# Starting a chunk's q preparation twelve attention units before its first use, in place of ten

## The chip, the cores and the metric

The kernel runs on one core of one Trainium2 chip. The metric is the device time of one execution in microseconds (us). The kernel before took 984.87 us (median of three runs, 982.25 to 988.37). One more execution was profiled; its numbers are used wherever a stage or an instruction is spoken of.

## The reference

Four batches, eight heads, 768 positions, head size 64. Attention lets a query see only the keys whose nearest centroid (of sixteen per head, by cosine) is the query's own; the attention output, 3072 rows of 512, then goes through an MLP with 2048 hidden columns and a squared ReLU.

```python
q_assign = np.argmax(np.einsum('bhsd,hcd->bhsc', q_n, c_n), axis=-1)
k_assign = np.argmax(np.einsum('bhsd,hcd->bhsc', k_n, c_n), axis=-1)
mask = q_assign[:, :, :, None] == k_assign[:, :, None, :]
scores = np.where(mask, scale * np.matmul(q, k.transpose(0, 1, 3, 2)), -1000000000.0)
attn = softmax(scores)                      # exp after subtracting the row maximum
x = (attn @ v).transpose(0, 2, 1, 3).reshape(B * S, H * D)
r = np.maximum(x @ w_in, 0.0)
out = (s * (r * r) + b) @ w_out
```

All of it is float32. The kernel works with pairs of float16 tiles, a high part and the remainder, so a product costs two or three matmuls.

## The kernel before, in words

**Units and steps.** Attention is cut into 192 units, each 128 queries of one head against all 768 keys. A chunk is 256 positions of one batch, so a batch has three chunks of 16 units and lasts 48 units. A chunk's q is prepared in two halves of four heads each; a half serves 8 units and is called a q group here (24 of them, numbered u = 0 to 23; group u serves units 8u to 8u+7). The MLP of a chunk is cut into 16 steps, one for each 128 hidden columns, 192 in all, and MLP step m is written into the same pass of the main loop as unit m + 21.

**One pass i of the main loop** (the `while` near the end of the function) writes: the scores of unit i (L456: two matmuls of QA by KA, then two of QB by KB, into `sc`, which has two buffers); output matmuls of an MLP step (L602, `acc`); the float16 copy of unit i-1's probabilities (L119, `ph`); the row maximum on VectorE (L465) and exp on ScalarE (L472, L475) of unit i; the input matmuls of an MLP step (L575, `h`, one PSUM bank) and its ReLU and squares on ScalarE (L582 to L585), which need the chunk's scale `cf`; the remainder of `ph` on GpSimd (L498) and its DMA transpose `PT` (L500); the remainder of `g` on GpSimd (L590); in every second pass the matmuls with v (L517 to L519, `px`) and their evacuation on VectorE (L525 to L529). Last comes `background()`, which advances every preparation in progress by one stage, up to its next `yield`.

**A q group's preparation** (`prep_q`) has eight stages and so takes eight passes: 1 load of `qn` (SP queue); 2 absolute maximum (VectorE, L101); 3 the maximum over partitions (PE `am_q` and VectorE L98, PSUM bank `m`); 4 seven small scale instructions on VectorE (L68 to L70, L362 to L64) and the high split on ScalarE (L185); 5 the remainder split on VectorE (L187), a copy on GpSimd (L375) and the DMA transpose `QA` (L379); 6 nothing; 7 matmuls with the centroids (`pq`, L388 and L389, bank `m`) and the first two one-hot instructions (L288, L289); 8 the other four (L291 to L294) and the DMA transpose `QB` (L392). The scores of the group's first unit need QA and QB, each of which has two buffers.

**Other background work.** For batches 1 to 3, `prep_k` of four head pairs begins at passes 48b-20, 48b-16, 48b-12 and 48b-8 with the same eight stages (and bank `m`), and `prep_v` begins at 48b-20. `finish_x` turns every four units' output into the MLP's input: first an absolute maximum (VectorE) in a pass that is 3 modulo 4, then, one pass later, a remainder on GpSimd and the transpose `x` (L546); after a chunk's last head pair also the maximum over partitions `am_x`, in passes 20, 36, 52 and so on (16n+20). `mlp_start`, one pass after that, turns `am_x` into `cf` with small VectorE instructions (L560 to L566). Bank `m` is one buffer shared by `px`, `am_q`, `am_k`, `am_v`, `am_x`, `pq` and `pk`.

**What sets the order.** The kernel says what is computed, and in which order it is written; a scheduler with a simulated clock then fixes each engine's instruction order, by order of writing where it can, and adds the waits. On the chip each engine runs its own list in that order. Loads are ordered behind the latest `PT` transpose on SP. In the first 24 units the weights are also loaded, checked and split (`weights`, `wsplit`), with VectorE at work most of the time.

Of the kernel before, what the change touches and what calls it, by code (L numbers as in the profile page):

```python
# [26 lines left out]
def tile_cluster_attention_mlp(ctx, tc, q, k, v, cent, w_in, w_out, s_in, b_in, out):  # L27
# [7 lines left out]
    NCH = T // CT  # L35
# [363 lines left out]
    def prep_v(b):  # L399
        vm = sb.tile([P, 8], F32, tag="vm", name=f"vm_{b}", bufs=2)  # L400
        VM[b] = vm
        vns = []
        for hp in range(NP):
            vn = sb.tile([P, 2, T, D], F32, tag="kv", name=f"vn_{b}_{hp}", bufs=5)
            load(vn, v[b, 2 * hp : 2 * hp + 2].rearrange("h (p t) d -> p h t d", t=T), False)
            vns.append(vn)
            if b == 0:
                VN[hp] = vn
            yield
        for hp in range(NP):  # L410
            absmax(vm[:, hp : hp + 1], vns[hp].rearrange("p h t d -> p (h t d)"))
            if hp < NP - 1:
                yield
        vc = columns(1, f"v{b}")
        V.tensor_reduce(vc, vm[:, 0:NP], axis=AX.X, op=ALU.max)
        if b:
            yield
        allmax(vm[:, 5:6], vc, f"v{b}")
        yield
        floor2(V, vm[:, 6:7], vm[:, 5:6])  # L420
        inverse2(V, vm[:, 7:8], vm[:, 6:7], 0)
        V.tensor_scalar(vm[:, 7:8], vm[:, 7:8], 2.0 ** 13, None, op0=ALU.mult)
        V.tensor_scalar(vm[:, 6:7], vm[:, 6:7], 2.0 ** -19, None, op0=ALU.mult)
        for hp in range(NP):
            vh = sb.tile([P, 2, T, D + 2], F16, tag="vh", name=f"vh_{b}_{hp}", bufs=5)
            vl = sb.tile([P, 2, T, D], F16, tag="vl", name=f"vl_{b}_{hp}", bufs=5)
            VS[(b, hp)] = (vh, vl)
            G.memset(vh[:, :, :, D:], 1.0)
            yield from split(vh[:, :, :, :D], vl, vns[hp], vm[:, 7:8], False)
            if hp < NP - 1:  # L430
                yield
                if b > 0:
                    yield
                    yield
# [184 lines left out]
    def at(step, gen):  # L619
        later.setdefault(step, []).append(gen)  # L620
# [8 lines left out]
    for b in range(B):  # L629
        for c in range(NCH):  # L630
            for hq in range(2):
                s0 = ((b * NCH + c) * 2 + hq) * 8 - 10
                if s0 > 0:
                    at(s0, prep_q(b, c, hq))
        if b > 0:
            for hp in range(NP):
                at(48 * b - 20 + 4 * hp, prep_k(b, hp))
            at(48 * b - 20, prep_v(b))
# [122 lines left out]
```

## Time and profile before

| | |
|---|---|
| time, median of three | 984.87 us (982.25 to 988.37) |
| profiled execution, its own time | 987.78 us |
| its span | 986.0 us |
| granted TensorE clock over the span | 0.941 |
| PE, ACT, DVE, POOL busy | 85%, 74%, 68%, 56% |
| first scores of unit 32 | about 208 us into the span |
| last scores of unit 191 | about 906 us into the span |

PE is TensorE, DVE VectorE, ACT ScalarE, POOL GpSimd and SP the queue that issues all DMAs here; PEld is the loading of weights into TensorE, beside its matmuls. A group's row in the profile gives how many instructions it has, their busy time in us, the mean of one in ns, and then the time for which the engine stood idle just before them with what ended that. Rows of a stage view give its length and each engine's busy time with the number of instructions.

### The profile page before, as it was taken

How to read it: one execution, taken by the hardware profiler on the slowest of the kernel's cores; microseconds unless marked ns; L12 is line 12 of the kernel's file. 1: busy time of each engine (PE TensorE's matmuls, PEld its weight loads, DVE VectorE, ACT ScalarE, POOL GpSimd, SP SyncE). 2: the span in 40 equal slices, each digit the busy share in tenths (PEclk: the TensorE clock that was granted, in tenths of full speed). 3: DMA queues.
4: the chain of work that ended last, by engine and by line, in shares of the span. 5: the costliest groups of instructions: out<-in, count | busy, mean ns of one | idle time of the engine just before them, and what ended most of it. 6: DMA issues, size and time to landing. Idle time of an engine off the chain costs nothing. (4 is left out here: it accounts for less than half of the span.)

```text
span 986.0 us, 22497 instructions
## 1 busy us (share of the span) xinstructions
PE 834.3 (85%) x8625; PEld 580.2 (59%) x8625; DVE 673.0 (68%) x1475; ACT 726.4 (74%) x1416; POOL 550.2 (56%) x543
## 2 busy tenths in 40 slices
PE   0568524887899999998799999997889999999997
PEld 0347312654566666765566666765666666767764
DVE  7798889989687665658787756578867567473100
ACT  4476776877578788867678877876788977789443
POOL 3125755556456576655467656655566766667322
PEclk9955566999999999999999999999999999999999
DMA  6865883687678775698888767797888676777200
GB/s 181 204 196 158 222 210 90 138 194 134 128 144 163 156 161 123 140 210 154 171 164 156 169 132 156 138 203 181 138 160 173 151 119 142 142 138 149 44 23 21
DMA packets 450299, 147.36 MB, mean 149 GB/s; under 512 B 417936, under 2 KB 446608, under 8 KB 450192
## 3 DMA queue, kind: packets, MB, share of 16 engines
q1 hardware_dynamic: 450192, 145.93, 69.7%
q8 instruction: 67, 1.10, 0.5%
q14 instruction: 40, 0.33, 0.1%
HBM read 35.69 MB, written 6.29 MB: 43 GB/s over the span
## 5 line engine op out<-in xcount | busy, mean ns | idle before, releaser
L498 POOL TENSOR_TENSOR ph<-p,ph 128x768 f16<-128x768 f32 x184 | 308.6, 1677 | 170.7 <-ACT ph L119 135.8
L575 PE MATMUL h<-x,wis 128*128 128x256 f16 x2304 | 292.0, 275 | 17.3 <-ACT r L582 12.2
L602 PE MATMUL acc<-wos,g 128*128 128x512 f16 x1152 | 295.4, 380 | 4.7 <-POOL g L590 2.9
L575 PEld LDWEIGHTS <-wis 128*128 128x128 f16 x2304 | 223.1, 98 | 74.9 <-issue 16.6
L590 POOL TENSOR_TENSOR g<-r,g 128x256 f16<-128x256 f32 x192 | 133.3, 695 | 139.7 <-ACT r L585 129.8
L465 DVE TENSOR_REDUCE ssm<-sc 128x1 f32<-128x768 f32 x192 | 180.9, 950 | 16.2 <-PE sc L456 16.0
L475 ACT ACTIVATE p<-sc,ssm,qsm 128x768 f32<-128x768 f32 x192 | 188.1, 980 | 3.9 <-DMA PT<-ph 1.8
L602 PEld LDWEIGHTS <-g 128*128 128x128 f16 x1152 | 104.1, 98 | 88.2 <-POOL g L590 6.9
L119 ACT ACTIVATE ph<-p 128x768 f16<-128x768 f32 x174 | 144.8, 832 | 11.1 <-DMA PT<-ph 10.8
L472 ACT ACTIVATE ssm<-ssm,lift,qsm 128x1 f32<-128x1 f32 x192 | 73.4, 382 | 101.9 <-DVE ssm L465 101.4
L517 PE MATMUL px<-vh,PT 128*128 128x65 f16 x1104 | 119.9, 196 | 14.5 <-DVE ksm L98 5.2
L582 ACT ACTIVATE r<-h,cf 128x256 f32<-128x256 f32 x192 | 89.1, 464 | 55.0 <-PE h L575 50.8
L518 PE MATMUL px<-vl,PT 128*128 128x64 f16 x1104 | 119.9, 193 | 0.0
L519 PE MATMUL px<-vh,PT 128*128 128x65 f16 x1104 | 119.9, 194 | 0.0
L456 PE MATMUL sc<-KA,QA 128*128 128x384 f16 x384 | 101.1, 343 | 20.2 <-ACT p L475 16.9
L518 PEld LDWEIGHTS <-PT 128*128 128x128 f16 x1104 | 103.6, 100 | 21.2 <-issue 12.8
L517 PEld LDWEIGHTS <-PT 128*128 128x128 f16 x1104 | 103.9, 98 | 17.5 <-issue 9.1
L456 PE MATMUL sc<-KB,QB 128*128 128x384 f16 x384 | 100.2, 345 | 7.8 <-DMA QB<-qb 7.7
L519 PEld LDWEIGHTS <-PT 128*128 128x128 f16 x1104 | 103.6, 98 | 3.0
L584 ACT ACTIVATE g<-r 128x256 f16<-128x256 f32 x192 | 79.5, 414 | 3.8
L585 ACT ACTIVATE r<-r 128x256 f32<-128x256 f32 x192 | 79.1, 412 | 3.3
L525 DVE TENSOR_SCALAR ssm<-px 128x2 f32<-128x2 f32 x92 | 14.2, 155 | 88.3 <-PE px L519 88.2
(153 smaller groups left out, 1090.9 us busy)
## 6 DMA issues: line engine op xcount, KB each, us to landing
wst<-in_moe_w_in_dram SPq DMA_DIRECT2D x16, 512.0 KB, 4.5
wst<-in_moe_w_out_dram SPq DMA_DIRECT2D x16, 512.0 KB, 4.1
kn<-in_k_dram SPq DMA_DIRECT2D x16, 384.0 KB, 3.9
qn<-in_q_dram SPq DMA_DIRECT2D x24, 256.0 KB, 3.8
vn<-in_v_dram SPq DMA_DIRECT2D x16, 384.0 KB, 4.4
out_dram<-o SPq DMA_DIRECT2D x12, 512.0 KB, 3.2
PT<-ph SPq DMA_TRANSPOSE x184, 3.4
x<-xn SPq DMA_TRANSPOSE x48, 2.5
```

Of the source, the lines that this page charges most:

```text
L119: A.activation(dst, src, AF.Copy)
L456: last_score[0] = nc.tensor.matmul(sc[:, e, :HALF], X[:, col, :], y[:, h * S + e * HALF : h * S + (e + 1) * HALF], start=st, stop=not st)
L465: last_max[0] = V.tensor_reduce(SM[i // 4][:, 0, j : j + 1], U[i]["sc"], axis=AX.XY, op=ALU.max, negate=True)
L475: last_exp[0] = A.activation(p.rearrange("p (a b) -> p a b", a=2), u["sc"], AF.Exp, bias=bi, scale=u["scale"], **total)
L498: G.tensor_tensor(u["ph"][:, 1, :], u["p"], u["ph"][:, 0, :], op=ALU.subtract)
L517: nc.tensor.matmul(o1, PT[:, kt, :], vh[:, h, kt, : D + 1], start=(kt == 0), stop=False)
L518: nc.tensor.matmul(o, PT[:, kt, :], vl[:, h, kt, :], start=False, stop=False)
L519: nc.tensor.matmul(o1, PT[:, T + kt, :], vh[:, h, kt, : D + 1], start=False, stop=(kt == T - 1))
L575: nc.tensor.matmul(ph[:, :CW], WSP[ft][0][:, wl, kt, :], XS[(b, c, kt)][:, :, xl, :], start=(i == 0), stop=(i == len(terms) - 1))
L582: A.activation(r, ph[:, :CW], AF.Relu, scale=MS[(b, c)][0])
L590: G.tensor_tensor(g[:, 1, :], r, g[:, 0, :], op=ALU.subtract)
L602: nc.tensor.matmul(acc[:, t, :], g[:, gl, rows], WSP[ft][1][:, wl, :], start=(ft == 0 and gl + wl == 0), stop=(ft == NF - 1 and gl == 1))
```

## The change

`prep_q` of group u is entered into the list of background work at pass 8u-12 in place of 8u-10. Only groups with a positive start are entered this way; u = 0 and u = 1 are prepared by hand ahead of the loop and in its first passes, before and after alike, so 22 groups move. No instruction is added or taken away; each of the eight stages is written two passes earlier.

```diff
     for b in range(B):
         for c in range(NCH):
             for hq in range(2):
-                s0 = ((b * NCH + c) * 2 + hq) * 8 - 10
+                s0 = ((b * NCH + c) * 2 + hq) * 8 - 12
                 if s0 > 0:
                     at(s0, prep_q(b, c, hq))
         if b > 0:
             for hp in range(NP):
                 at(48 * b - 20 + 4 * hp, prep_k(b, hp))
             at(48 * b - 20, prep_v(b))
```

`at(step, gen)` keeps a list for each pass; the main loop appends that list to the active preparations when it reaches the pass, and `background()` advances them in the order in which they were appended.

## The prediction

> **What bounds the kernel now.** I read the page first, then the stages, then PE's waits, then single stretches around a q group's first use, a chunk's start and a change of batch.
>
> ```profile
> span 986.0 us, 22497 instructions
> ...
> PE 834.3 (85%) x8625; PEld 580.2 (59%) x8625; DVE 673.0 (68%) x1475; ACT 726.4 (74%) x1416; POOL 550.2 (56%) x543
> ...
> PE   0568524887899999998799999997889999999997
> ...
> DVE  7798889989687665658787756578867567473100
> ```
>
> PE is the busiest engine and its slices say where: from the eighth on (after some 170 us) nearly all are 8 or 9; before, PE has room and DVE is the fuller engine. The stages put numbers to it: one row from the point where attention is in full swing to the last scores, one from the MLP's tail, one from the stage ahead.
>
> ```profile
> 177.00:906.00 729.00, 674.37 (x7334) 468.46 (x7333) 511.83 (x1126) 576.32 (x1122) 447.15 (x417) 0.99 0.76 154
> ...
> 941.00:976.00 35.00, 34.89 (x239) 23.38 (x239) 0.06 (x1) 17.76 (x41) 8.72 (x13) 1.00 0.04 16
> ```
> ```profile
> 127.00:177.00 50.00, 19.96 (x188) 12.46 (x188) 45.04 (x88) 32.86 (x57) 27.11 (x20) 0.60 0.59 155
> ```
>
> The columns after the length are PE, PEld, DVE, ACT, POOL. In the tail PE runs without a break, 34.89 of 35. From 177 to 906 us it is idle for 729.00 - 674.37 = 54.6 us; whatever the change does there, it can win no more than that. The clock column is 0.99 and 1.00 there, so no term comes from it. What PE waits for between 177 and 906 us (waits by engine, PE alone: total, times, longest):
>
> ```profile
> PE h L575 <- ACT r L582: 12.2, 10, 3.1
> PE sc L456 <- ACT p L475: 8.3, 8, 1.8
> PE sc L456 <- DMA QB<-qb: 5.8, 7, 2.0
> ...
> PE px L517 <- DVE xm L98: 2.6, 5, 0.8
> ```
>
> QB is third here; with the waits of the weight loads it is first. The tile view of QB for the same stretch:
>
> ```profile
>   DMA QB<-qb: 14.6, 15
> ...
>   PEld L456: 8.8, 8
>   PE sc L456: 5.8, 7
> ```
>
> **The change part by part.** Nothing is added or removed; 22 groups have their eight stages written two passes earlier. What moves per group, from rows of 177 to 906 us (20 groups):
>
> ```profile
> L185 ACT ACTIVATE qb<-qn,qsm 128x256 f16<-128x256 f32 x40 | 18.1, 498 | 4.9 <-DVE qsm L362 4.5
> ...
> L375 POOL COPY qa<-qb 128x512 f16<-128x512 f16 x20 | 15.4, 769 | 0.0
> L101 DVE TENSOR_REDUCE amb_q<-qn 128x2 bf16<-128x512 f32 x20 | 13.7, 684 | 38.7 <-DMA qn<-in_q_dram 38.7
> L294 DVE TENSOR_SCALAR qb<-oo_q 128x512 f16<-128x512 f16 x20 | 13.1, 654 | 0.3
> ...
> L288 DVE TENSOR_REDUCE om_q<-pq 128x8 f32<-128x128 f32 x20 | 5.8, 288 | 25.3 <-PE pq L389 25.2
> ```
> ```profile
> qn<-in_q_dram SPq DMA_DIRECT2D x24, 256.0 KB, 3.8
> ...
> QA<-qa SPq DMA_TRANSPOSE x24, 2.9
> ```
>
> and, for the DVE instructions that touch `qsm` (stages 3, 4 and the remainder split) and then those that touch `oe_q` (the other one-hots):
>
> ```profile
> 177.00:906.00 729.00, 94.14 (x180) 241.74 (x374) 0.99 0.76 154
> ```
> ```profile
> 177.00:906.00 729.00, 39.54 (x80) 0.99 0.76 154
> ```
>
> DVE per group: (13.7 + 94.14 + 5.8 + 39.54 + 13.1) / 20 = 8.3 us. ScalarE two splits of 0.50, GpSimd one copy of 0.77; on SP one load and two transposes. The load and its reader stay one pass apart, so the 38.7 us that DVE waits for `qn`, and the 25.2 for `pq`, have no reason to change in total: 0, and DVE isn't the end of the chain over most of the span.
>
> *QB's wait.* Around 609 us, SP's queue, then PE's scores:
>
> ```profile
> 608.91 1.27 SPq L392 DMA_TRANSPOSE QB<-qb  x1
> 610.27 1.15 SPq L85 DMA_DIRECT2D qn<-in_q_dram  x1
> ```
> ```profile
> 606.59 0.48 PE L456 MATMUL sc<-KA,QA 128*128 128x384 f16 x2
> 612.89 0.50 PE L456 MATMUL sc<-KB,QB 128*128 128x384 f16 x2 [0.77 <-DMA QB<-qb]
> ```
>
> The first unit's QA half was done at 607.1; its QB half waited in one of the two score buffers until 612.89, behind a transpose issued at 608.91. Two passes are about 2 x 729 / 160 units = 9 us (units 32 to 191 in that stretch), more than the 6.3 us gap. So this wait goes, at most 14.6 us in all, at least nothing if the score is late for its buffer anyway: the row `sc <- ACT p` (8.3 us) is what stands next. I take half, 7.3: 5.8 of it stops matmuls, 8.8 only weight loads, behind which matmuls may still run.
>
> *A chunk's start.* With ten passes, stage 7 of every second group falls into pass 16n+20, where `finish_x` makes `am_x`, and stage 8 into 16n+21, beside `mlp_start`. DVE's list near 467 us, then PE:
>
> ```profile
> 467.32 0.29 DVE L289 TENSOR_TENSOR oe_q<-pq,om_q 128x128 f32<-128x128 f32 x1
> 467.64 1.69 DVE L291 TENSOR_TENSOR oe_q<-oe_q,rev 128x128 f32<-128x128 f32 x1
> 469.25 0.28 DVE L98 TENSOR_REDUCE xm<-am_x 128x1 f32<-128x128 f32 x1
> 469.45 0.27 DVE L292 TENSOR_REDUCE om_q<-oe_q 128x8 f32<-128x128 f32 x1
> ...
> 469.76 0.28 DVE L293 TENSOR_TENSOR oo_q<-oe_q,om_q 128x128 f16<-128x128 f32 x1
> ...
> 470.68 1.02 DVE L294 TENSOR_SCALAR qb<-oo_q 128x512 f16<-128x512 f16 x1
> ...
> 474.34 0.19 DVE L564 TENSOR_SCALAR cf<-xm,glob 128x1 f32<-128x1 f32 x1
> ```
> ```profile
> 475.18 1.03 PE L575 MATMUL h<-x,wis 128*128 128x256 f16 x8 [3.05 <-ACT r L582]
> ```
>
> The q's one-hots (1.69 + 0.27 + 0.28 + 1.02 = 3.3 us) stand between x's maximum and `cf`; the ReLU waits for `cf`, the only `h` bank for the ReLU, and PE stops 3.05 us. With twelve passes stages 7 and 8 are at 16n+18 and 16n+19; only the load stands at 16n+20. What is late next is x's own path: the maximum over its tile is in pass 16n+19, now behind stage 8's 2.3 us of one-hots, but has a pass (4.6 us) in hand. I take the two long waits, 3.05 and the longest of the row, 3.1: a gain of 6.1; ends 12.2 (all ten) and nothing. The GpSimd copy and the QA transpose now meet `finish_x`'s own in passes 0 modulo 4; 0.77 us there, hidden by a PE that isn't fed by them until a pass later.
>
> *A change of batch.* K's four preparations start at 48b-20, -16, -12, -8; the q groups of the same stretch started at 48b-18, -10, -2, between them, and now start at 48b-20, -12, -4. Two groups run in step with a head pair's eight stages; the third meets one only in its stages 3 and 4, 2.8 us (`qsm` without the remainder splits: stage 4's are 40 instructions of 0.98, so (94.14 - 39.4) / 20 = 2.7). Displaced onto k's own DVE work: 2 x 8.3 + 2.7 = 19.3 us a change, 58 us over three. In the six stages around the changes (first, last, sum):
>
> ```profile
> 218.00:257.00 39.00, 29.80 (x328) 19.39 (x327) 38.49 (x90) 29.45 (x55) 22.72 (x18) 0.96 0.77 153
> ...
> 679.00:723.00 44.00, 38.40 (x439) 27.39 (x438) 34.72 (x78) 32.79 (x64) 24.69 (x25) 1.00 0.81 161
> sum 249.00, PE 216.78 PEld 149.21 DVE 200.22 ACT 182.71 POOL 140.97; mean PE 36.13 PEld 24.87 DVE 33.37 ACT 30.45 POOL 23.49
> ```
>
> DVE is busy 200.22 of 249.00, and PE idle 249.00 - 216.78 = 32.2, or 0.16 us for each us of DVE work. Queued behind two one-hot chains at once are the next row maxima, on which exp and so the score buffers wait. At that rate 58 us displaced cost 9.3 us. Ends: the idle time doubles, +32; or a gain of 2.6, since `pq` also leaves pass 48b-12, where `am_x` and `am_v` share its bank (row `px <- DVE xm`).
>
> *The first 177 us.* Groups 2 to 4 move among weight splits, DVE 45.04 of 50 us busy. No work is added: 0, with one load's landing (3.8 us) for each of three groups either way, 11 us.
>
> Sum: -7.3 - 6.1 + 9.3 = -4.1. The profiled execution took 987.78 us, 1.8 beyond its span, so 983.7; it lies 2.9 above the median of 984.87, so against that **981 us**.
>
> **The rivals.**
>
> *Faster:* QB's wait goes whole (14.6), the starts give 6.1, and DVE's free fifth at the batch changes absorbs the collisions: -20.7, 964 us. For it: 48.8 idle us of DVE in those six stages; against: in 218 to 257 DVE has 0.5 us left. The Trainium skill (DMA: Bandwidth & Descriptors, Rules for kernel authors) says to issue a transfer early and wait for it late, so that its fixed cost is overlapped; by that the whole QB term goes. The trace agrees at 609 us, where the issue came after the use, but bears nothing out about what DVE does meanwhile.
>
> *Slower:* the batch changes. Two one-hot chains and two scale chains in one pass hold back the row maxima, bank `m` must serve `pq` and `pk` and `am_k` between two `px`, and each displaced us costs 0.32 of PE, twice the rate above: +18.6; with the starts giving nothing and half of QB, +11.3, 996 us. It decides from 5.7 us lost a change (17.2 in all, 7.3 + 1% of 985). At the far end, idle time doubled, +25, 1010 us.
>
> *Nothing happens:* QB's repeated gap could be a shortage of its two buffers, so that an earlier transpose only waits for its slot. The Trainium skill (Perfetto Trace Analysis, Optimization Strategy) reads the same gap repeating as a possible shortage of buffers; by that the time stays 985 us. Against it, the slot's last reader is unit 8u-9, and QA's write now falls in pass 8u-8, QB's in 8u-5; at 609 us it was the data that came late.
>
> **How the numbers follow.** Forecast 0.45, faster rival 0.30, slower 0.22, nothing 0.03. About 1% (9.8 us) is what a measurement of this kernel can tell from no change. The forecast and the last case lie within it: faster 0.30, same 0.48, slower 0.22. The range goes from the faster rival's 964 to 1000, the slower one's 996 and some of its tail; the rest of that tail, and a gain of all ten chunk starts as well, are left out with about 0.17. The forecast's own range is 975 to 990.
>
> **What would show it.** Right: QB's row of waits near nothing; no q one-hot between `xm<-am_x` and `cf`; PE's wait for ACT's ReLU below 7 us. The stages around 48b-20 to 48b show more PE idle than 32 us if the collisions cost, and more waits of ACT for the row maxima. Wrong: the QB waits gone and PE idle as before (another gate took their place), a changed start of the first 177 us by over 11 us, or a stage away from both places that differs by more than a few us.

## The result, and the profile after

The changed kernel took 994.19 us (median of seven runs) beside 986.70 us for the kernel before: a ratio of 1.0101, 95% interval 1.0065 to 1.0137. It is slower by 1%, some 10 us by that ratio (the medians are 7.5 us apart). The forecast was 981 us, a small gain. The page of the profiled execution (992.5 us of span against 986.0), the lines that answer those shown of before:

```profile
span 992.5 us, 22541 instructions
...
PE 838.5 (84%) x8625; PEld 583.8 (59%) x8625; DVE 669.6 (67%) x1475; ACT 726.7 (73%) x1416; POOL 559.3 (56%) x543
...
PE   1565435988699799998899799988998999999997
...
DVE  7799798989675765756867765767778556553110
...
PEclk9967555999799899999799999998999999999999
```

Between the profiled executions PE is busy 4.2 us longer for the same matmuls (838.5 against 834.3) and idle 2.3 us longer. The clock line has a 7 in slices where the line of before has nines. The row from 177 to 906 us, after:

```profile
177.00:906.00 729.00, 673.46 (x7254) 468.53 (x7254) 503.96 (x1111) 568.29 (x1107) 450.28 (x413) 0.97 0.74 152
```

In this stretch PE is idle 729.00 - 673.46 = 55.5 us, where it was 54.6 before, and has done 80 matmuls fewer. This is the sign that the prediction gave for a failure: QB's waits gone, and PE idle as before.

Where time went shows in a count. The view of stages, restricted to the row maxima (one DVE instruction of L465 for each attention unit), before and then after; the first stage holds the first change of batch, the third and the fifth hold the second and the third:

```profile
177.00:340.00 163.00, 32.17 (x34) 0.97 0.77 151
340.00:480.00 140.00, 29.14 (x31) 1.00 0.77 160
480.00:535.00 55.00, 12.51 (x14) 1.00 0.79 148
535.00:690.00 155.00, 33.72 (x36) 1.00 0.79 164
690.00:740.00 50.00, 10.08 (x11) 1.00 0.83 151
```
```profile
177.00:340.00 163.00, 26.85 (x29) 0.95 0.64 137
340.00:480.00 140.00, 31.12 (x33) 0.99 0.77 152
480.00:535.00 55.00, 8.73 (x10) 0.91 0.71 151
535.00:690.00 155.00, 36.49 (x39) 1.00 0.81 165
690.00:740.00 50.00, 8.57 (x9) 0.91 0.79 154
```

At the changes of batch 5, 4 and 2 units fewer are done in the same time; between them 2 and 3 more. So the change does both things: it wins between the changes and loses more at them. At about 4.6 us a unit these differences are 50 us lost and 23 won; that overstates both, since PE also has the MLP's work to do, but the places are plain. (Up to 177 us the changed kernel has done 26 units, the one before 23. The stretches are equal in time and do not hold the same units.)

From 177 us on, QB's waits are gone (ahead of that, PE's waits for it grew from 1.9 to 6.7 us). The tile view of QB, 177 to 906 us, has no wait for its DMA left; its last line is the row maxima waiting for the score matmuls, which was 12.4 us before:

```profile
its engine sat idle before it (us, times) until:
  issue: 1.4, 8
who waited for it (us, times):
  DVE ssm L465: 29.8, 36
```

In their place stand others. PE's waits in the same stretch, with total, times and longest:

```profile
PE sc L456 <- ACT p L475: 10.2, 13, 1.9
PE h L575 <- DMA x<-xn: 7.7, 5, 3.9
PE am_x L97 <- DVE amb_x L550: 6.8, 5, 2.6
PE h L575 <- ACT r L582: 6.1, 9, 1.5
...
PE am_v L97 <- DVE xs L529: 3.6, 3, 1.4
PE pk L338 <- DVE xs L529: 2.9, 2, 1.7
```

The waits for `x` and `amb_x`, at the MLP's chunk starts, weren't among the rows of before. `am_v` and `pk` wait for the evacuation of `px`, that is for bank `m`. One place at the second change of batch, in the order of time (PE's instructions that waited, then four of DVE):

```profile
479.77 0.23 PE L97 MATMUL am_v<-identb,amb_v 128*128 128x128 bf16 x1 [1.45 <-DVE xs L529]
...
480.48 0.23 PE L97 MATMUL am_x<-identb,amb_x 128*128 128x128 bf16 x1 [0.49 <-DVE amb_x L550]
...
481.10 0.21 PE L517 MATMUL px<-vh,PT 128*128 128x65 f16 x1 [0.38 <-DVE vm L64]
...
483.87 0.80 PE L575 MATMUL h<-x,wis 128*128 128x256 f16 x3 [0.66 <-DMA x<-xn]
...
486.33 0.17 PE L338 MATMUL pk<-cT,KA 128*128 128x16 f16 x1 [1.67 <-DVE xs L529]
```
```profile
483.33 2.26 DVE L187 SCALAR_TENSOR_TENSOR vl<-vn,vm,vh 128x768 f16<-128x768 f32 x1
485.51 0.21 DVE L566 SCALAR_TENSOR_TENSOR xm<-xm,glob 128x1 f32<-128x1 f32 x1
485.64 0.15 DVE L526 RECIPROCAL ssm<-ssm 128x2 f32<-128x2 f32 x1
485.90 0.29 DVE L529 TENSOR_TENSOR xs<-px,ssm 128x128 f32<-128x128 f32 x1
```

`am_v`, `am_x`, `px` and `pk` follow one another through the one buffer of bank `m`, each after VectorE has read the one before; and `xs`, which frees the bank for `pk`, stands behind a 2.26 us instruction of v's preparation. The stages around this place, after and then before (PE, PEld, DVE, ACT, POOL, granted clock):

```profile
470.90:481.00 10.10, 7.71 (x74) 4.59 (x73) 8.50 (x25) 5.17 (x10) 3.76 (x4) 0.98 0.76 177
481.00:491.20 10.20, 7.78 (x81) 5.55 (x81) 8.42 (x24) 6.77 (x11) 5.69 (x4) 0.51 0.80 200
```
```profile
462.90:473.10 10.20, 6.94 (x85) 4.59 (x84) 9.69 (x26) 6.87 (x11) 7.01 (x6) 1.00 0.73 154
473.10:483.30 10.20, 8.12 (x79) 5.91 (x79) 6.41 (x18) 5.81 (x13) 3.65 (x4) 1.00 0.97 206
```

After, the clock was granted at 0.51 for the ten microseconds that follow; before, at 1.00. PE doesn't stand longer here than before: over the two rows it is idle 20.30 - 15.49 = 4.8 us, and 20.40 - 15.06 = 5.3 before. It has done 155 matmuls in place of 164, and of PE's columns it is the clock that stands out. The four users of bank `m` here are v's, x's, the products' and k's; q's own two are not among them. So the place shows how the bank is handed on, and not q meeting k in it.

### The profile page after: what moved, and what is told of

The parts are those of the page before. It is cut to its first block, busy times and chain, and to the rows that moved or that the text cites. A ratio compares the mean times of both kernels' runs of the same rounds, so it can differ in the third digit from the quotient of the medians.

```text
span 992.5 us, 22541 instructions
## 1 busy us (share of the span) xinstructions
PE 838.5 (84%) x8625; PEld 583.8 (59%) x8625; DVE 669.6 (67%) x1475; ACT 726.7 (73%) x1416; POOL 559.3 (56%) x543
## 4 chain that ended last, share of the span: by engine, by line
PE 44%; DVE 20%; DMA 14%; ACT 7%; issue 6%; POOL 6%; SPq 2%; POOLq 0%; DVEq 0%; ACTq 0%
PE h L575 15%; PE acc L602 14%; PE sc L456 6%; DVE ssm L465 4%; POOL ph L498 4%; DMA wst<-in_moe_w_out_dram 2%; PE px L517 2%; DMA qn<-in_q_dram 2%; PE px L519 2%; PE px L518 2%; DMA QA<-qa 2%; DMA vn<-in_v_dram 2%; ACT p L475 1%; DVE qa L187 1%; POOL g L590 1%
## 5 line engine op out<-in xcount | busy, mean ns | idle before, releaser
L465 DVE TENSOR_REDUCE ssm<-sc 128x1 f32<-128x768 f32 x192 | 181.1, 950 | 32.5 <-PE sc L456 32.0
L517 PE MATMUL px<-vh,PT 128*128 128x65 f16 x1104 | 124.5, 199 | 15.4 <-DVE qsm L98 4.8
L518 PE MATMUL px<-vl,PT 128*128 128x64 f16 x1104 | 124.6, 196 | 0.0
L519 PE MATMUL px<-vh,PT 128*128 128x65 f16 x1104 | 124.1, 197 | 0.0
L456 PE MATMUL sc<-KA,QA 128*128 128x384 f16 x384 | 102.3, 348 | 21.4 <-ACT p L475 18.4
L518 PEld LDWEIGHTS <-PT 128*128 128x128 f16 x1104 | 105.7, 101 | 21.5 <-issue 12.6
L517 PEld LDWEIGHTS <-PT 128*128 128x128 f16 x1104 | 105.9, 100 | 18.2 <-issue 5.7
L456 PE MATMUL sc<-KB,QB 128*128 128x384 f16 x384 | 102.7, 349 | 6.7 <-DMA QB<-qb 6.7
L519 PEld LDWEIGHTS <-PT 128*128 128x128 f16 x1104 | 106.0, 100 | 3.8
```

The lines of the kernel that those rows point to most:

```text
L456: last_score[0] = nc.tensor.matmul(sc[:, e, :HALF], X[:, col, :], y[:, h * S + e * HALF : h * S + (e + 1) * HALF], start=st, stop=not st)
L465: last_max[0] = V.tensor_reduce(SM[i // 4][:, 0, j : j + 1], U[i]["sc"], axis=AX.XY, op=ALU.max, negate=True)
L517: nc.tensor.matmul(o1, PT[:, kt, :], vh[:, h, kt, : D + 1], start=(kt == 0), stop=False)
L518: nc.tensor.matmul(o, PT[:, kt, :], vl[:, h, kt, :], start=False, stop=False)
L519: nc.tensor.matmul(o1, PT[:, T + kt, :], vh[:, h, kt, : D + 1], start=False, stop=(kt == T - 1))
```

## The experiments

"Out of step" means that a q group's stages and k's are two passes apart (or one), "in step" that they fall into the same passes. Ratios are to the kernel before, run beside them. Where an edit adds lines, the line numbers in that run's views are higher by as many (L457 of one view is L456 of another). First, where the loss sits, and whether it is the phase.

**Twelve passes only away from the changes, and only around them.**

```diff
+                near = ((b * NCH + c) * 2 + hq) % 6 in (5, 0, 1)
-                s0 = ((b * NCH + c) * 2 + hq) * 8 - 10
+                s0 = ((b * NCH + c) * 2 + hq) * 8 - (10 if near else 12)     # the first run
+                s0 = ((b * NCH + c) * 2 + hq) * 8 - (12 if near else 10)     # the second run
```

> Twelve passes ahead for the q groups away from a change of batch, ten for the three around each change (u modulo 6 in 5, 0, 1). Theory A (the loss sits at the changes of batch, where the q stages fall in step with k's; elsewhere twelve is a gain): the changes cost as in the kernel before, the rest keeps the gain of some 9 us a batch that the two traces show, so 965 to 980 us. Rival B (twelve costs wherever it stands, the place is chance of the scheduler's order): about as slow as all twelve, 988 to 996 us.

> The other half alone: twelve passes for the three groups around each change, ten for the rest. Theory A: the loss of 7 to 18 us a change without the gain between, 1000 to 1015 us. Rival B: between the two kernels, 987 to 994 us.

Measured: 981.51 us (0.9934, 0.9905 to 0.9963) and 1006.21 us (1.0202, 1.0156 to 1.0248). Away from the changes (12 of the 22 groups) twelve wins 6.5 us, around them it costs 18 to 20. The sum of the two, +1.4%, is near the change's +1.0%. Theory A holds, though the first run's gain is smaller than it expected.

**Moving k instead.** Both kernels with k's preparations two passes later; in the first q is at twelve (out of step), in the second at ten (in step).

```diff
-                at(48 * b - 20 + 4 * hp, prep_k(b, hp))
+                at(48 * b - 18 + 4 * hp, prep_k(b, hp))
```

> All q groups twelve passes ahead, and k's four preparations at 48b-18 and on in place of 48b-20, so q and k stand two passes apart again as in the kernel before. Theory A (being in step is what costs): faster than the kernel before, 965 to 980 us. Rival B (q earlier costs whatever k does, or k later costs too): 990 to 1000 us.

> q ten passes ahead as before, k's four preparations at 48b-18 and on: q isn't moved at all, but now stands in step with k. Theory A: slower than the kernel before, 1000 to 1015 us. Rival B (q's earlier place is what costs): 985 to 990 us.

Measured: 970.55 us (0.9827, 0.9793 to 0.9862) and 1003.42 us (1.0153, 1.0110 to 1.0197). The second kernel doesn't move q at all and is slow; the first moves q as the change does and is faster than both kernels.

**q still earlier.** Fourteen passes, k as before: two apart from k again. And thirteen: one apart.

```diff
-                s0 = ((b * NCH + c) * 2 + hq) * 8 - 10
+                s0 = ((b * NCH + c) * 2 + hq) * 8 - 14     # and - 13
```

> All q groups fourteen passes ahead, k as before: q is moved still further, but stands two passes apart from k again (48b-22, -14, -6 against 48b-20, -16, -12, -8). Theory A (the phase against k decides): 965 to 982 us, faster than the kernel before. Rival B (the earlier, the worse): over 995 us.

> All q groups thirteen passes ahead, k as before: q stands one pass (modulo 4) from k's stages, and its stages 3 and 7, with bank m, fall into the odd passes in which the products with v use bank m. If only the meeting with k counts: 968 to 982 us. If any other user of bank m in the same pass counts as much: 985 to 1000 us.

Measured: 970.58 us (0.9819, 0.9797 to 0.9840) and 975.31 us (0.9857, 0.9822 to 0.9892). Between thirteen and twelve lie 2.4%, some 24 us, and of ten, twelve, thirteen and fourteen twelve is the only one in step with k. At thirteen, stages 3 and 7 fall into the passes of `px`, another user of bank `m`, and the kernel is only 0.4% slower than at fourteen. Rival B, that q's earlier place costs by itself, has fallen.

PE's waits in the kernel with q at twelve and k at 48b-18, 177 to 880 us:

```profile
PE sc L456 <- ACT p L475: 14.0, 18, 1.4
PE acc L602 <- POOL g L590: 5.9, 8, 1.0
PE h L575 <- DMA x<-xn: 3.0, 3, 1.4
```

The row for `x` has fallen from 7.7 us to 3.0, and the ones for `am_v` and for `am_x <- amb_x` are no longer among the larger rows.

**Which stages.** Around the changes alone, twelve passes, with a pause of two passes after stage 2, 3 or 6 (two more `yield`s at that place in `prep_q`), so that the later stages are written where ten puts them.

> As the run with twelve passes around the changes alone (1006 us), but those groups pause two passes after stage 2: only the load and the absolute maximum stand in step with k, stages 3 to 8 stand where they stand with ten. If the loss comes from the three loads in one pass (q, k, v on one queue): 1000 to 1010 us. If it comes from VectorE's work or bank m: 985 to 991 us, as the kernel before.

> The same with the pause after stage 3: load, absolute maximum and the maximum over partitions in step, stages 4 to 8 as with ten. If bank m is what costs, a part of the loss shows here, 992 to 1000 us; if VectorE's long stages are, 985 to 991 us.

> The same with the pause after stage 6: stages 1 to 5 in step, the centroid matmuls, the one-hots and QB's transpose as with ten. If the one-hot stages (7 and 8, VectorE and bank m) are what costs: 985 to 992 us; if the scale and split stages are: 998 to 1008 us.

Measured: 998.68 (1.0112), 988.72 (0.9997) and 995.44 us (1.0062), against 1006.21 (1.0202) with all eight in step. The first and the third lie between the ranges expected. The second lies in the one that speaks for VectorE's long stages, but this isn't a staircase: with stage 3 in step too, the kernel is faster than with the first two alone. Between the third and all eight in step lie 1.4%, which is the cost of stages 7 and 8 less what the earlier QB wins. But an edit of this kind can evidently shift the whole order by 10 us, so these three runs do not tell which stage costs.

**Bank m.** The partition maximum and the centroid matmuls of the q groups around the changes go into the MLP's bank `h`, in the changed kernel and in the one out of step (q at twelve, k at 48b-18).

```diff
+        other = b + c == 0 or (b * 6 + c * 2 + hq) % 6 in (5, 0, 1)
-        allmax(sm[:, 1, :], qm, f"q{n}", "m" if b or c else "h")
+        allmax(sm[:, 1, :], qm, f"q{n}", "h" if other else "m")
-        pa = (ps_m if b or c else ps_h).tile([P, 512], F32, tag="m" if b or c else "h", name=f"pq_{n}")
+        pa = (ps_h if other else ps_m).tile([P, 512], F32, tag="h" if other else "m", name=f"pq_{n}")
```

> The changed kernel (q twelve ahead, in step with k), with the partition maximum and the centroid matmuls of the three q groups around each change put into the MLP's PSUM bank h in place of the shared bank m. If being in step costs through bank m: 970 to 985 us. If it costs through VectorE's order: 992 to 1002 us.

> The same move of those two stages into bank h in the kernel that is out of step (q twelve ahead, k at 48b-18, 970.6 us): what the move costs or gains by itself. Bank m theory: 968 to 976 us, so little of its own; if it gains as much here as in the kernel in step, the gain isn't the phase's.

Measured: 985.24 us (0.9958, 0.9940 to 0.9975) and 978.60 us (0.9898, 0.9873 to 0.9923). The first is at the edge of the range for bank `m`, the second 3 us beyond its own. In step the move wins 1.4%, out of step it costs 0.7%. The price of being in step, 2.7% with the shared bank (1.0101 against 0.9827), is 0.6% with the bank apart. In step, PE's waits of `am_v` and of `am_x <- amb_x` leave the list, and k's centroid matmuls now wait for their own transpose instead:

```profile
PE pk L338 <- DMA KA<-ka: 11.6, 4, 3.9
PE sc L457 <- ACT p L476: 9.6, 10, 2.6
PE h L576 <- ACT r L583: 5.6, 8, 1.8
```

PE's own waits don't show the meeting in the bank clearly. Those of the bank's users for VectorE, other than for an operand of their own (`amb_x`, `amb_q`), add up from 177 to 890 us to 17.2 us in the changed kernel and 19.8 and 23.5 in the two others in step (around the changes alone; q at ten with k later); they are 17.8 in the kernel before and 13.7 and 16.4 out of step (k at 48b-18; q at fourteen). They lean the right way, but the changed kernel has no more of them than the one before.

**VectorE.** The remainder split of the same groups leaves VectorE for ScalarE and GpSimd, in both kernels.

```diff
-... sm[:, 2, j : j + 1], b + c == 0))
+... sm[:, 2, j : j + 1], b + c == 0 or (b * 6 + c * 2 + hq) % 6 in (5, 0, 1)))
```

> The changed kernel with the split of the three q groups around each change done by ScalarE and GpSimd, as batch 0's first groups do it: VectorE is relieved of two instructions of about 0.98 us a group, of 8.3 us. If VectorE's load in the passes in step is what costs: 982 to 989 us. If bank m's order is: 992 to 998 us.

> The split of the three q groups around each change on ScalarE and GpSimd, in the kernel out of step (q twelve ahead, k at 48b-18, 970.6 us). In step this move cost some 9 us. If it costs as much here (978 to 986 us), the cost is the move's own, and the run in step says that VectorE's relief is worth nothing; if it costs nothing here (968 to 974 us), GpSimd or ScalarE is the engine that suffers from being in step.

Measured: 1008.96 us (1.0189, 1.0155 to 1.0224) and 995.84 us (1.0066, 1.0041 to 1.0091). Both are slower than any range expected. The edit costs 0.9% in step and 2.4% out of step. The lines of the engines' busy time from the two pages:

```profile
PE 848.8 (84%) x8625; PEld 587.3 (58%) x8625; DVE 652.8 (65%) x1455; ACT 731.7 (73%) x1436; POOL 568.2 (56%) x563
```
```profile
PE 844.4 (85%) x8625; PEld 587.4 (59%) x8625; DVE 650.4 (65%) x1455; ACT 732.3 (74%) x1436; POOL 567.9 (57%) x563
```

DVE is 17 us less busy than in the kernels they come from (669.6 and 667.5), and both are slower. So less work on VectorE, bought with work on two other engines, is no gain. It doesn't clear VectorE, though. By the measure used for the bank, the price of being in step is 1.2% with this edit (1.0189 against 1.0066), in place of 2.7%: this edit too takes away a good part of it, if not as much as the other bank does.

**QB late.** In the kernel with q at twelve and k at 48b-18, QB's transpose is written two passes later; in a second run it is also ordered behind the probabilities' transpose of that pass.

```diff
         yield from onehot(pa, nh * CT, f"q{n}", mk, BIG, 0.0)
-        nc.sync.dma_start_transpose(QB, ...)
+        yield
+        yield
+        with behind(last_transpose[0]):          # the second run only
+            nc.sync.dma_start_transpose(QB, ...)
```

> The kernel with q twelve passes ahead and k at 48b-18 (970.6 us), with the QB transpose of every group held back two passes: all other stages stay early, QB comes as late as with ten. If the 18 us that kernel wins over the one before are mostly QB's wait: back to 980 to 988 us. If they come from the other stages' places: 968 to 975 us.

> The run that only wrote QB's transpose two passes later left it on the chip where it was, some 14 us ahead of its use, since the scheduler pulled it forward. Here it is also tied behind the probabilities' transpose of its pass, in the kernel with q twelve ahead and k at 48b-18 (970.6 us), so it lands as late as with ten, some 5 us after its issue. If QB's wait is worth something like the 14.6 us named in the prediction's faster case: 980 to 988 us; if half, as forecast: 975 to 980 us; if nothing: 968 to 974 us, with the scheduler's own scatter of some 5 us on top.

Measured: 975.89 us (0.9875, 0.9846 to 0.9905) and 990.31 us (1.0017, 0.9989 to 1.0045). The first is just above the range for the other stages' places, the second above all of its ranges. In the first run QB's transpose was still issued 9 to 16 us ahead of its use in most groups, as without the edit, so it says nothing of QB, and its 5 us are what an edit can do that leaves QB where it was. In the second it was issued 3 to 8 us ahead in nearly all, as in the kernel before, and the waits are back (tile view of QB, 177 to 910 us):

```profile
  DMA QB<-qb: 11.3, 5
...
  PEld L459: 6.2, 3
  PE sc L459: 5.1, 2
```

Out of step, an early QB is worth 1.4% (against the first of these two runs) to 1.9% (against the kernel without either edit), 14 to 19 us: most or all of what this kernel wins over the one before. The waits that name QB are 11.3 us of it. The order behind the probabilities' transpose is new as well, and PE is busy 843.1 us in the second run, 838.2 in the first and 832.9 without the edits, so not all of it need be QB's.

Nor does a late QB always make PE wait: with q at ten and k at 48b-18 its transpose is issued 3 to 9 us ahead of its use, as in the kernel before, and QB's tile view from 177 to 915 us has no wait for the DMA either.

**The clock.** Twelve matmuls whose result nobody reads, ahead of the MLP's first input matmuls of six chunks, in the changed kernel.

```diff
+        if ft == 0 and (b * 3 + c) in (1, 2, 4, 5, 7, 8):
+            for _ in range(12):
+                nc.tensor.matmul(ph[:, CW:], WSP[0][0][:, 0, 0, :], WSP[0][1][:, 0, :CW], start=True, stop=True)
```

> The changed kernel with twelve matmuls of 256 columns, whose result nobody reads, ahead of the MLP's first input matmuls in six chunk starts (those around the changes): 1.3 us of TensorE work each where TensorE waits for x, 8 us in all. If the halved clock after those waits costs several us: fewer stretches at half clock and 985 to 991 us. If the halved clock costs nothing, since TensorE isn't what is late there: 993 to 1003 us.

Measured: 999.98 us (1.0119, 1.0071 to 1.0168), no different from the changed kernel's 1.0101. The mean clock from 177 to 915 us is 0.97 in both. That is in the range for a clock that costs nothing, but the run doesn't price it, since the added work didn't come where PE waits: in its trace the twelve matmuls run 10 to 16 us ahead of the input matmul of their chunk that needs the last `x` (in one chunk at 470.30 us, where that matmul starts at 480.04).

Busy and idle time say more. With q at fourteen PE is busy 839.7 of 970.6 us, as long as in the changed kernel (838.5 of 992.5), and idle 130.9 us in place of 154.0. With k at 48b-18 it is busy 832.9 of 968.2 us, so 18.7 of the 24.3 us between that kernel and the changed one are idle time. What sets the kernels in step apart from those out of step is mostly idle time, and not matmuls at a lower clock. Between the changed kernel and the one before it is the other way round: 4.2 of 6.5 us are busy time.

## Why the prediction was wrong

*What bounds the kernel.* Right in the main: from 177 to 906 us PE is busy for all but 55 us, before and after. But "no term comes from it", of the clock, was read from the kernel before; in the changed one the clock falls to half at several places after 177 us, and PE is busy 4.2 us longer.

*QB's wait (forecast -7.3, ends 0 and -14.6) and a chunk's start (forecast -6.1).* Both mechanisms were right. QB lands well ahead of its use and no wait for it is left after 177 us. (At 609 us QB's issue, 608.91, came after the QA half of the score, and not after the use of QB, 612.89, as the faster rival has it.) The ReLU's waits fell from 12.2 us to 6.1, and at the place shown no one-hot stands between `xm<-am_x` and `cf` any longer. What the two are worth together is read from the kernels out of step (k at 48b-18, and q at fourteen): 1.7 to 1.8%, some 17 us, against 13.4 forecast. Away from the changes, 12 of the 22 groups won 6.5 us, where their share of the 13.4 is 7.3. So the two terms were some 4 us too small at most. How they divide isn't shown; a late QB cost 14 to 19 us when it was put back. That a late QB holds a score buffer, and with it the maxima and exps behind it, would explain more than its named waits, but is argued only.

In step the starts were no gain: PE waits 7.7 us for `x` and 6.8 for `amb_x`, more than the ReLU's waits fell by, so x's own path did not have the pass in hand that the prediction gave it. With q at the same place and k two passes later `x` is 3.0, the ReLU 0.6, and no wait for `amb_x` is left. So this too belongs to the meeting with k.

*A change of batch (forecast +9.3, ends -2.6 and +32).* This is the step that failed. It took the displaced VectorE work, 58 us, at 0.16 us of PE idle for each, an average of idle to busy time that no row ties to displaced work. Measured around the changes alone: +18 to +20 us, with the gains of those groups inside it; between q at twelve out of step and in step, 2.7%, 27 us. The two agree: with the ten groups' share of the 17 us of gain, 8, the first is 26 to 28 as well. That is 0.47 us for each us displaced, three times the rate. So the forecast's -13.4 and +9.3 stand beside -17 and +27.

What the 27 us are made of is shown in part. The cost needs q and k in step: moving either one alone costs 1.0 or 1.5%, moving both wins 1.7%. With q's two users of bank `m` in the MLP's bank, 0.6 of the 2.7% is left; with the remainder split off VectorE, 1.2%. So the shared bank, which the term counted only as a possible gain and the slower rival named as a cost, has the larger effect, but the bank is handed on by VectorE's readers, and these runs don't divide the cost between the two. Each edit also makes a new order, and one that left QB where it was moved the time by 5 us.

*The slower rival* had the place, and a cost (+18.6, deciding from 17.2) nearer the measured one. That its total of 996 us is so near 994 is partly luck: its gain (7.3) and its cost were both too small, by about as much. The forecast's end of +32 did hold the measured cost, so the term's range was right where its middle, and with it the sign of the sum, was wrong.

*The first 177 us (forecast 0, ends -11 and +11).* The changed kernel is three units ahead at 177 us, and reaches unit 24 about 7 us earlier; that much was won and lost again at the first change.

*The other rivals.* The faster one (QB's wait whole, the collisions absorbed) is near what the kernels out of step do: 0.982 to 0.986. The Trainium skill's rule to issue a transfer early and wait late (DMA: Bandwidth & Descriptors, Rules for kernel authors) agrees with the runs there: putting QB back late cost 1.4 to 1.9%. It says nothing of what the move meets on its way. "Nothing happens" fell: QB's waits ended, and the time moved.

What stays open: how the cost of being in step divides between bank `m`, VectorE and the order that the scheduler makes of them; why 0.6% is left with the bank apart; and what the halved clock costs by itself.

## What to carry to other kernels

Moving a preparation earlier moves it into other company: list, pass by pass, which other streams then use the same single-buffered tile, and prefer an offset out of phase with them (here 13 or 14 passes, or k moved along, beat the kernel before by 1.4 to 1.8%). Waits that name one tile can all go and leave the engine as idle as it was: here 14.6 us of QB's waits went, and PE's idle time from 177 to 906 us stayed at 55 us. An average of idle to busy time is no price for work that is moved to another place. An edit of the writing order counts only where the trace shows that the order on the chip followed it; QB's transpose, written two passes later, was still issued where it had been.

## What the runs showed of the hardware

The TensorE clock fell to 0.51 for about 10 us after a stretch in which PE was busy 7.71 of 10.10 us and its longest listed wait was 1.45 us; waits of 1.45, 0.49 and 0.38 us stood within 2.8 us at its end. Twelve input matmuls took 2.77 us at that clock (from 488.21 us) and 1.47 at full clock (in the kernel before, from 478.38 us). In the kernel before the clock stayed at 1.00 through a stretch of 4.76 us busy of 10.10 (465.1 to 475.2 us) that ends with a wait of 3.05 us, and for the ten microseconds behind it. The Trainium skill (TensorE: Matmul & The Clock Gate, HAM oscillation) gives idle gaps of more than some 3.4 us as what to avoid. In these traces the clock fell after shorter ones and held after one nearly as long, so neither the longest gap nor the busy share alone told when it would.
